# One core, a grouped-query decode step with a gated feed-forward branch: q turned on VectorE, whole-row products in the down and output projections, the first set reordered

## The chip, the cores and the metric

The kernel runs on one core of one Trainium2 chip. The metric is device time in microseconds (us) of one execution. The core has five engines with queues of their own: TensorE (PE in the profile, with its weight loads as PEld), VectorE (DVE), ScalarE (ACT), GpSimd (POOL) and SyncE (SP), which here issues every transfer. They meet only through semaphores.

## What is computed

One decode step for a batch of four, over 32 query heads in 8 groups and the last 4096 of 16384 cached positions, beside a gated feed-forward branch; a sigmoid mixes the two.

```python
g = sigmoid((x * gate_w).sum(-1, keepdims=True))            # x: 4 x 1 x 512
q = (x @ wq)                                                # 32 heads of 128
k, v = k_cache[:, :, Sk - W:, :], v_cache[:, :, Sk - W:, :] # W = 4096, 8 heads, each for 4 query heads
p = softmax(einsum("bhqd,bhkd->bhqk", q, k) * 128 ** -0.5)
a = einsum("bhqk,bhkd->bhqd", p, v).reshape(4, 1, 4096) @ wo
gate, up = x @ W_gate, x @ W_up                             # 512 x 1792
b = (gate * (gate > 0) * up) @ W_down                       # 1792 x 512
return g * a + (1 - g) * b
```

All inputs are bf16. K and V of the window are 67 MB of the 81 MB that are read.

## The kernel before

**Sets and slots.** The work is cut into eight sets, one batch row with four of the eight key heads each: 4 MB of K and 4 MB of V. SBUF has four slots of 4 MB. V always takes slot 3; wq, the K tiles, the gate and up weights, the down weights and wo take slots 0 to 2 in turn. `_dma_order` (L159) is the order on SyncE's queue: wq, x, gate_w, K0, K1, V0, and then K(s), V(s-1) pair by pair, the feed-forward weights around the last V, and wo in five pieces (`WO_PIECES`, L26, in units of half a row group of 256 columns). A load waits until its slot is free (`_slots`, L166): V(s) for the value product of set s-1, K for the scores of the K that lay there. Whatever stands behind a waiting issue waits too.

**The start.** Constants for masks and sums are made on POOL and TensorE (`CONST`). `XT` turns x on TensorE; `Z` is the product for the gate's sigmoid; `Q` is x @ wq in 32 products of four rows, four column groups side by side, into two banks. The rows of q must come to lie as block-diagonal weights `qblk`. Before, `EQ` (L554 on VectorE, L658 on ScalarE) copies each bank four times over, `QT` (L339) turns the result in 16 fp32 transposes on TensorE, and `EQT` (L564) puts it into place in 16 copies out of PSUM.

**A set.** VectorE transposes a quarter of K in 32x32 blocks (`EKT`, called KT in the order; 128x2048 as fp32 pairs); TensorE multiplies it with `qblk` (`SC`, eight products of 512 columns for a quarter); VectorE adds the mask, takes the maximum and writes the scores to SBUF (`ESC`, L584). After four quarters `MAX` and a small TensorE product (`SW`) give each row its maximum; ScalarE takes the exponential of all 2048 columns (`EXP`, L687); VectorE transposes the result (`EPT`, called PT, L599); TensorE forms the value product (`PV`, 32 products in two column groups); ScalarE copies it to `osb` (`NORM`, L672). VectorE's order is written out in `_order` (L148). TensorE's is a loop whose blocks are shared by all sets: scores of quarters 0 and 1, value product of the set before, scores of quarters 2 and 3, `SW`.

**The end.** `RS` sums the exponentials by row. `GU` multiplies x with the gate and up weights; RELU, `H` and `EHT` make the hidden activations and turn them. Then come the last value product, `FFN` (L408, down projection), `OQ` (L385, which folds the value products of all sets into the layout of the output projection by 16 products with 0/1 weights), `EOQ` (L608, scaling), and `WO` (L416). FFN and WO add into one PSUM bank: each row group of 512 output columns is two products of 256 columns, one in rows 0 to 3 and one in rows 64 to 67, in two column groups of the array. `FIN` copies both halves to SBUF and the result goes out.

The wait that orders the value tiles is this line of `_slots`:

```python
frees[n] = {"k": [("E", "SC", it[-1], 2)], "v": [("PV", it[-1])], "wq": [("Q", 1)], ...}[k]
```

Of the kernel before, what the change touches and what calls it, by code (L numbers as in the profile page):

```python
# [11 lines left out]
B = 4  # L12
# [12 lines left out]
OR = 128 // OUTT  # L25
WO_PIECES = ((0, 35), (35, 52), (52, 59), (59, 62), (62, 64))  # L26
# [78 lines left out]
def _alloc(nc, ctx):  # L105
# [13 lines left out]
    sb("osb", [128, NSET, 512], BF16)  # L119
    sb("oq", [128, 32, 4], BF16)  # L120
    sb("identb", [128, 128], BF16)
    sb("identf", [128, 128], FP32)
# [11 lines left out]
    sb("fold", [128, 4, 4, 64], BF16)  # L134
# [4 lines left out]
    sb("recip", [128, 4, 4], FP32)  # L139
# [8 lines left out]
def _order():  # L148
    o = [("CONST", k) for k in ("mask", "grp", "rfold")] + [("XT",), ("Z",), ("Q",), ("QT",), ("KT", 0, 0), ("KT", 0, 1), ("SC", 0, 0)]
    o += [("KT", 0, 2), ("SC", 0, 1), ("KT", 0, 3), ("SC", 0, 2), ("SC", 0, 3), ("SW", 0)]  # L150
    for s in range(1, NSET):
        o += [("KT", s, 0), ("KT", s, 1), ("PT", s - 1), ("SC", s, 0), ("KT", s, 2), ("SC", s, 1), ("KT", s, 3), ("PV", s - 1)]
# [35 lines left out]
def _program(nc, plan, R, aps):  # L188
# [3 lines left out]
    TR, SCB, ACC, OB = (0, 1), (2, 3), 5, 6  # L192
    slots, kt, sc, pe, pT, qblk = R["slots"], R["kt"], R["sc"], R["pe"], R["pT"], R["qblk"]
    xsb, xT, osb, oq = R["xsb"], R["xT"], R["osb"], R["oq"]
    identb, identf, ones = R["identb"], R["identf"], R["ones"]
# [17 lines left out]
    turns = [("CONST", k) for k in consts] + [("XT",)] + [("QT", n, x) for n in range(2) for x in range(2)]  # L213
    bank_of = {key: TR[i % 2] for i, key in enumerate(turns)}
    bank_of.update({("Q", 0): 2, ("Q", 1): 3, ("RS", 0): 0, ("RS", 1): 1, ("GU", 0): 2, ("GU", 1): 3, ("OQ",): 4})
# [4 lines left out]
    free = {("RS", 0): [("E", "SW", NSET - 1)], ("RS", 1): [], ("GU", 0): [("E", "SC", NSET - 1, 2)],  # L220
# [51 lines left out]
    def gpsimd(e):  # L272
# [12 lines left out]
        aff(identf[:, :], ones[:, :], [[-1, 128]], 0, eq, 0.0, ("IDF",))  # L285
# [11 lines left out]
        for g in range(8):  # L297
            v = R["fold"][:, g % 4, :, :]
            aff(v, v, [[1, 4], [-1, 64]], -64 * g, ne, 1.0, ("FOLD", g), mult=4)

    def tensor(t):
# [37 lines left out]
        def QT():  # L339
            for n in range(2):  # L340
                for x in range(2):
                    key = ("QT", n, x)
                    for y in range(4):
                        src = qd(n)[:, 512 * x + 128 * y:512 * x + 128 * y + 128]
                        tp(banks[tr(key)][:, 128 * y:128 * (y + 1)], src, identf[:, :], ev=key if y == 3 else None,
                           waits=tr_free(key) + [("QD", n), ("IDF",)])

# [19 lines left out]
        def RS(g):  # L367
            key = ("RS", g)
            mm(banks[tr(key)][:, 0:4], R["rfold"][:, :], rowsum[:, 4 * g:4 * g + 4], True, True, ev=key,
               waits=tr_free(key) + [("EXP", 4 * g + 3), ("E", "CONST", "rfold")])  # L370
# [14 lines left out]
        def OQ():  # L385
            key = ("OQ",)
            if plan.emit:
                E.take("nm", 1)
            for t in range(2):
                for cc in range(2):  # L390
                    for c in range(4):
                        x = 256 * t + 128 * cc + 32 * c
                        first, lastmm = (t, cc, c) == (0, 0, 0), (t, cc, c) == (1, 1, 3)
                        mm(banks[tr(key)][0:64, 0:256], R["fold"][:, 2 * cc + t, c, :], osb[:, :, x:x + 32], first, lastmm,
                           ev=key if lastmm else None, pos=(0, 0),
                           waits=tr_free(key) + [("FOLD", 7)] if first else ())

        def GU():
            for n, (W, key) in enumerate(((Wg, "WG"), (Wu, "WU"))):
# [8 lines left out]
        def FFN():  # L408
            for i in range(14):
                for j in range(OUTT):  # L410
                    x = 512 * i + OW * j
                    mm(banks[ACC][OR * j:OR * j + 4, 0:OW], R["hg"][:, i, :], Wd[:, x:x + OW], i == 0, False,
                       ev=("FFN",) if (i, j) == (13, OUTT - 1) else None, waits=[("E", "HT"), ("WD",), ("G",)],
                       pos=(0, OR * j))

        def WO(p):  # L416
            lo, hi = WO_PIECES[p]
            w = [("WO", p), ("E", "OQ")]
            for x in range(lo, hi):
                i, j = x // OUTT, x % OUTT  # L420
                mm(banks[ACC][OR * j:OR * j + 4, 0:OW], oq[:, i, :], Wo[:, OW * x:OW * x + OW], False, i == 31,
                   ev=("WOP", p) if x == hi - 1 else None, waits=w if x == lo else (), pos=(0, OR * j))

        fns = dict(CONST=CONST, XT=XT, Z=Z, Q=Q, QT=QT, SC=SC, PV=PV, SW=SW, RS=RS, OQ=OQ, WO=WO, GU=GU, FFN=FFN)
# [6 lines left out]
        def setup():  # L431
            run("CONST", "XT", "Z", "Q", "QT")
            E.wait([("E", "QT", n, 1) for n in range(2)] + [("E", "CONST", "grp")])

        if not plan.emit:
# [9 lines left out]
            run("FFN", "OQ", "WO")  # L445
# [38 lines left out]
        with block("mix"):  # L484
            run("FFN", "OQ")
            for p in range(len(WO_PIECES) - 1):
                WO(p)
            t.br("pe_tail")
# [6 lines left out]
    for it in order:  # L495
# [10 lines left out]
        elif k == "Q":  # L506
            dve += [("EQ", 0), ("G",)]
            act.append(("EQ", 1))
        elif k == "QT":
            dve += [("EQT", 0), ("EQT", 1)]  # L510
# [8 lines left out]
        elif k == "PT":  # L519
            dve.append(("EPT", it[1]))  # L520
        elif k == "RS":
            dve.append(("ERS", it[1]))
        elif k == "PV":
            act.append(("NORM", it[1]))
        elif k == "OQ":
            dve.append(("EOQ",))
    dve.append(("FIN",))
    act.append(("FIN",))

    def qd(n):  # L530
        return (pe, sc)[n][:, :].bitcast(FP32)

    def q_dst(n, u):
        return (pe, sc)[n][:, :].rearrange("p (x u w) -> p x u w", x=8, u=4)[:, :, u, :]

    def q_src(n):
        return banks[scb(("Q", n))].rearrange("p (x w) -> p x w", x=8)

    def vector(v):
# [14 lines left out]
        def EQ(n):  # L554
            key = ("Q", n)
            E.op(lambda: v.tensor_copy(q_dst(n, 0), q_src(n)), ev=("E",) + key, waits=[key])
            E.op(lambda: v.tensor_copy(q_dst(n, slice(1, 4)), bc(q_dst(n, slice(0, 1)), 2, 3)), ev=("QD", n),
                 waits=[("E",) + key])
# [5 lines left out]
        def EQT(n):  # L564
            U32 = mybir.dt.uint32
            keys = [("QT", n, x) for x in range(2)]
            assert [tr(k) for k in keys] == list(TR)
            src = R["psum"][:, 0:2, :].bitcast(U32).rearrange("p k (h g j b) -> p g b j (k h)", h=2, g=2, j=4)
            for q in range(4):
                r = slice(32 * q, 32 * q + 32)  # L570
                for g in range(2):
                    dst = qblk[r, 4 * n:4 * n + 4, g, 16 + 32 * q:32 + 32 * q, :].rearrange("p b c e -> p b (c e)")
                    dst = dst.bitcast(U32).rearrange("p b (j h) -> p b j h", j=4)
                    E.op(lambda dst=dst, r=r, g=g: v.tensor_scalar(dst, src[r, g, 0:B, :, :], 0, None, op0=ALU.bitwise_or),  # L574
                         ev=("E",) + keys[1] if (q, g) == (3, 1) else None, waits=keys + [("QZ",)])
            plan.ev[("E",) + keys[0]] = plan.ev[("E",) + keys[1]]

        def ESC(s, f):
            key = ("SC", s, f)
            w = [key]  # L580
            if f == 0:
                w += [("EXP", s - 1)] if s > 0 else [("QT", 1, 1)]
# [19 lines left out]
        def ERS(g):  # L602
            key = ("RS", g)
            E.op(lambda: v.reciprocal(recip[:, 2 * g, :], banks[tr(key)][:, 0:4]), ev=("E",) + key, waits=[key])
            E.op(lambda: v.tensor_tensor(recip[:, 2 * g + 1, :], recip[:, 2 * g, :], gg[:, 0, :], ALU.mult), ev=("RG", g),
                 waits=[("E",) + key, ("G",)])

        def EOQ():  # L608
            key = ("OQ",)
            for g in range(2):  # L610
# [4 lines left out]
                    bc(recip[0:64, 2 * g + 1, :].unsqueeze(2), 2, 32), ALU.mult), ev=("E",) + key if g else None,  # L615
                    waits=[key, ("RG", 1)])
# [16 lines left out]
        def FIN():  # L633
            E.op(lambda: v.tensor_copy(osum[:, OW:2 * OW], banks[ACC][OR:OR + 4, 0:OW]), ev=("OSUM", 1),  # L634
                 waits=[("WOP", len(WO_PIECES) - 1)])

        fns = dict(INIT=INIT, EKT=EKT, EXT=EXT, EQ=EQ, G=G, EQT=EQT, ESC=ESC, MAX=MAX, ESW=ESW, EPT=EPT, ERS=ERS, EOQ=EOQ, H=H,
# [15 lines left out]
    def scalar(a):  # L653
        E = _Eng(plan, a, "act")

        def EQ(n):
            key = ("Q", n)
            E.op(lambda: a.activation(q_dst(n, slice(0, 4)), bc(q_src(n).unsqueeze(2), 2, 4), ACTF.Copy), ev=("QD", n),  # L658
                 waits=[key])
            plan.ev[("E", "Q", n)] = plan.ev[("QD", n)]  # L660
# [10 lines left out]
        def NORM(s):  # L671
            E.op(lambda: a.activation(osb[:, s, :], ob, ACTF.Copy), ev=("NORM", s), ctr="nm",  # L672
# [54 lines left out]
```

## Time and profile before

| | before |
|---|---|
| median of three runs | 197.69 us (196.96 to 198.31) |
| profiled execution, its own time | 197.25 us |
| its span, first to last instruction | 196.0 us |
| mean granted TensorE clock | 0.852 |
| PE, PEld busy | 125.8, 56.4 us |
| DVE, ACT, POOL busy | 124.7, 27.5, 9.5 us |
| read from HBM | 81.01 MB, 413 GB/s over the span |

The page divides the span into 40 equal slices and gives for each the busy share of the engines, the granted clock, the share of the 16 DMA engines and the rate. A timeline row reads: start, length, engine, line, operation, output and input, shapes, count, and in brackets how long the engine was idle before it and what ended that. Rows of equal instructions are merged, so a length covers all of them. A row of windows gives, for a stretch, its length and each engine's busy time with its count (PE, PEld, DVE, ACT, POOL), then the granted clock, the DMA share and GB/s. Matmuls and transposes go through helpers, so all have line 305 or 309 and are told apart by their tiles.

### The profile page before, as it was taken

What the parts mean: (1) busy time and instruction counts of PE and PEld (TensorE: products, weight loads), DVE (VectorE), ACT (ScalarE), POOL (GpSimd) and SP (SyncE); (2) the same over time, 40 slices, a digit from 0 to 9 for tenths busy, and PEclk for the clock granted to TensorE, in tenths of its full rate; (3) what the DMA queues carried; (4) which work ended last, traced back from release to release, by engine and by line L of the source; (5) the groups of instructions that cost most, each with busy time, mean ns of one, the idle gap of its engine ahead of it and who ended that gap; (6) DMA issues with size and microseconds to landing.
All of it is one profiled execution on the core that took longest, in us unless ns stands there. A gap on an engine that the chain in (4) does not pass through costs nothing. (4 is left out here: it accounts for less than half of the span.)

```text
span 196.0 us, 2003 instructions
## 1 busy us (share of the span) xinstructions
PE 125.8 (64%) x723; PEld 56.4 (29%) x723; DVE 124.7 (64%) x153; ACT 27.5 (14%) x34; POOL 9.5 (5%) x25
## 2 busy tenths in 40 slices
PE   0209356649938963896389546954795589563976
PEld 0004212213413421252125212511251125221563
DVE  6103688699679949963995399539954994371010
ACT  2212100040140003011301120112012201220100
POOL 7830000000000000000000000000000000000000
PEclk9999859957996995799669978995899579965799
DMA  6999999999599999999999999999999999999994
GB/s 214 441 442 448 435 438 428 448 428 428 214 421 448 435 435 428 428 428 428 428 428 428 428 428 428 428 428 428 428 428 428 455 420 430 447 441 395 433 409 156
DMA packets 3619, 81.03 MB, mean 413 GB/s; under 512 B 409, under 2 KB 674, under 8 KB 802
## 3 DMA queue, kind: packets, MB, share of 16 engines
q1 hardware_dynamic: 3618, 81.01, 96.7%
q8 instruction: 1, 0.02, 0.0%
HBM read 81.01 MB, written 0.00 MB: 413 GB/s over the span
## 5 line engine op out<-in xcount | busy, mean ns | idle before, releaser
L305 PE MATMUL bank<-kt,qblk 128*128 128x512 bf16 x256 | 75.0, 455 | 30.6 <-PEq L82 30.6
L548 DVE STREAM_TRANSPOSE kt<-slots 128x2048 f32<-128x2048 f32 x32 | 72.9, 2297 | 4.2 <-DMA slots<-in_A_k_cache_dram 4.1
L305 PEld LDWEIGHTS bank<-kt,qblk 128*128 x256 | 27.8, 111 | 74.2 <-issue 57.3
L584 DVE CUSTOM_DVE_ANT_0 sc<-bank,maskf 128x512 bf16<-128x512 f32 x32 | 21.5, 671 | 28.2 <-PE bank L305 28.2
L305 PE MATMUL bank<-slots,pT 128*64 128x512 bf16 x256 | 31.0, 397 | 10.9 <-PEq L82 10.9
L305 PEld LDWEIGHTS bank<-slots,pT 128*64 128x64 bf16 x256 | 16.8, 114 | 25.4 <-issue 16.8
L687 ACT ACTIVATE pe<-sc,negmax 128x2048 bf16<-128x2048 bf16 x8 | 16.0, 2002 | 50.7 <-DVE negmax L594 50.7
L599 DVE STREAM_TRANSPOSE pT<-pe 128x2048 bf16<-128x2048 bf16 x8 | 18.2, 2274 | 2.2 <-ACT pe L687 2.2
L672 ACT ACTIVATE osb<-bank 128x512 bf16<-128x512 f32 x8 | 4.8, 597 | 91.2 <-PE bank L305 91.2
L612 DVE TENSOR_TENSOR oq<-bank,recip 64x128 bf16<-64x128 f32 x2 | 0.9, 432 | 11.4 <-PE bank L305 11.4
L305 PE MATMUL bank<-rd,grpb 128*128 128x32 bf16 x8 | 1.4, 176 | 8.9 <-PEq L82 8.9
L305 PE MATMUL bank<-slots,xT 128*4 128x512 bf16 (+1 forms) x64 | 6.3, 564 | 0.0
L552 DVE COPY xT<-bank 128x20 bf16<-128x20 bf16 x1 | 0.2, 171 | 8.0 <-PE bank L309 8.0
L305 PE MATMUL bank<-slots,oq 128*4 128x256 bf16 x64 | 4.4, 272 | 1.1 <-DVE oq L612 1.1
L574 DVE TENSOR_SCALAR qblk<-bank 32x64 uint32<-32x64 uint32 x16 | 2.9, 215 | 3.0 <-PE bank L309 2.9
L305 PE MATMUL bank<-maskr,maskl 128*128 128x512 bf16 x1 | 0.6, 607 | 5.9 <-POOL maskr L281 5.9
L305 PEld LDWEIGHTS bank<-rd,grpb 128*128 128x128 bf16 x8 | 0.8, 96 | 12.6 <-issue 12.6
L309 PE MATMUL bank<-identb,xsb 5*128 5x5 bf16 x4 | 0.3, 168 | 5.9 <-DMA xsb<-in_gate_w_dram 5.9
L305 PEld LDWEIGHTS bank<-slots,oq 128*4 128x4 bf16 x64 | 2.7, 84 | 2.9 <-DMA slots<-in_A_wo_dram 2.4
L281 POOL TENSOR_SCALAR_AFFINE_SELECT fold<-fold 128x256 bf16<-128x256 bf16 x8 | 3.3, 417 | 1.1
L594 DVE TENSOR_REDUCE negmax<-bank 128x1 f32<-128x32 f32 x8 | 1.5, 191 | 2.9 <-PE bank L305 2.9
L634 DVE CAST xsb<-bank 4x256 bf16<-4x256 f32 x1 | 0.4, 419 | 4.6 <-PE bank L305 4.6
(59 smaller groups left out, 42.2 us busy)
## 6 DMA issues: line engine op xcount, KB each, us to landing
slots<-in_A_k_cache_dram SPq DMA_DIRECT2D x8, 4096.0 KB, 24.8
slots<-in_A_v_cache_dram SPq DMA_DIRECT2D x8, 4096.0 KB, 15.6
slots<-in_A_wq_dram SPq DMA_DIRECT2D x1, 4096.0 KB, 12.3
slots<-in_A_wo_dram SPq DMA_DIRECT2D x1, 2240.0 KB, 21.6
slots<-in_B_W_gate_dram SPq DMA_DIRECT2D x1, 1792.0 KB, 19.3
slots<-in_B_W_up_dram SPq DMA_DIRECT2D x1, 1792.0 KB, 23.0
slots<-in_B_W_down_dram SPq DMA_DIRECT2D x1, 1792.0 KB, 18.2
slots<-in_A_wo_dram SPq DMA_DIRECT2D x1, 1088.0 KB, 23.8
```

Of the source, the lines that this page charges most:

```text
L281: op(lambda: e.affine_select(dst, src, pattern, cmp, fill, base=base, channel_multiplier=mult), ev)
L305: E.op(lambda: t.matmul(out_, lhsT, rhs, start=start, stop=stop, tile_position=pos, skip_group_check=True), ev=ev, waits=waits)
L309: E.op(lambda: t.transpose(out_, in_, idn), ev=ev, waits=waits)
L548: E.op(lambda: v.transpose(kt[:, f % 2, :].bitcast(FP32), slot("k", s)[:, 4096 * f:4096 * f + 4096].bitcast(FP32)), ev=("E", "KT", s, f), ...
L574: E.op(lambda dst=dst, r=r, g=g: v.tensor_scalar(dst, src[r, g, 0:B, :, :], 0, None, op0=ALU.bitwise_or), ev=("E",) + keys[1] if (q, g) == ...
L584: E.op(lambda: v.tensor_tensor_reduce(sc[:, 512 * f:512 * f + 512], banks[scb(key)], R["maskf"][:, :], 1.0, -3.0e38, ALU.add, ALU.max, mx4 ...
L594: E.op(lambda: v.tensor_reduce(negmax[:, s % 2:s % 2 + 1], banks[tr(key)][:, 0:32], AXIS.X, ALU.min), ev=("E",) + key, waits=[key])
L599: E.op(lambda: v.transpose(pT[:, :], pe[:, :]), ev=("E", "PT", s), ctr="pt", waits=[("EXP", s)] + ([("PV", s - 1)] if s else []))
L612: E.op(lambda g=g, r=r: v.tensor_tensor(oq[r, :, :].rearrange("p i b -> p b i"), banks[tr(key)][0:64, 128 * g:128 * g + 128].rearrange("p ...
L634: E.op(lambda: v.tensor_copy(osum[:, OW:2 * OW], banks[ACC][OR:OR + 4, 0:OW]), ev=("OSUM", 1), waits=[("WOP", len(WO_PIECES) - 1)])
L672: E.op(lambda: a.activation(osb[:, s, :], ob, ACTF.Copy), ev=("NORM", s), ctr="nm", waits=[("PV", s)])
L687: E.op(lambda: a.activation(pe[:, :], sc[:, :], ACTF.Exp, bias=negmax[:, s % 2:s % 2 + 1], scale=SCALE, accum_out=rowsum[:, s:s + 1]), ev= ...
```

## The change

**q on VectorE.** Each bank of Q is copied once to bf16 (ScalarE one, VectorE one), transposed in 32x32 blocks as fp32 pairs (`TQ`), and put into `qblk` by 32 copies of 32x32 elements (`QB`). The 16 TensorE transposes, the fourfold copies and the fp32 identity are gone. `Q` goes ahead of `Z`, and `G` (the sigmoid's reciprocal) moves behind the first `EPT`.

**The first set.** The next set's first K transpose is put ahead of the first set's last score block, its maximum and `SW`.

**The fold.** `NORM` now packs the two halves of a set that matter into `osb` of half the width, in four copies of 32 rows; for the last set ScalarE does two and VectorE two. `OQ` needs 8 products instead of 16. `RS` is one product instead of two.

**Whole rows.** `FFN` forms 14 products of 512 columns in rows 0 to 3 of a bank of its own instead of 28 halves, and the first 12 of 32 row groups of wo (`WX`) likewise. The other 20 stay in halves: the left ones are added to the same rows 0 to 3, the right ones go to rows 64 to 67 of the old bank. So the right half of FFN and WX is copied aside (`XS`) before the left halves start, and added in `FIN`. In the first piece of wo all right halves go ahead of the left ones. `OQ` stands ahead of `FFN`. `GU` waits for the last `EPT`.

TensorE's program has 449 instructions in place of 551, weight loads and products counted apart.

```diff
-    o = [...] + [("XT",), ("Z",), ("Q",), ("QT",), ("KT", 0, 0), ("KT", 0, 1), ("SC", 0, 0)]
-    o += [("KT", 0, 2), ("SC", 0, 1), ("KT", 0, 3), ("SC", 0, 2), ("SC", 0, 3), ("SW", 0)]
+    o = [...] + [("XT",), ("Q",), ("Z",), ("KT", 0, 0), ("KT", 0, 1), ("SC", 0, 0)]
+    o += [("KT", 0, 2), ("SC", 0, 1), ("KT", 0, 3), ("SC", 0, 2)]
     for s in range(1, NSET):
-        o += [("KT", s, 0), ("KT", s, 1), ("PT", s - 1), ("SC", s, 0), ...]
+        o += [("KT", s, 0)] + [("SC", 0, 3), ("SW", 0)] * (s == 1) + [("KT", s, 1), ("PT", s - 1), ("SC", s, 0), ...]
...
-    o += [("PT", s), ("RS", 0), ("RS", 1), ("GU",), ("PV", s), ("FFN",), ("OQ",)]
+    o += [("PT", s), ("RS",), ("GU",), ("PV", s), ("OQ",), ("FFN",), ("WX",)]
...
         def GU():
+            if plan.emit:
+                E.take("pt", 1)
...
         def FFN():
             for i in range(14):
-                for j in range(OUTT):
-                    x = 512 * i + OW * j
-                    mm(banks[ACC][OR * j:OR * j + 4, 0:OW], R["hg"][:, i, :], Wd[:, x:x + OW], i == 0, False, ...)
+                mm(banks[ACX][0:4, :], R["hg"][:, i, :], Wd[:, 512 * i:512 * i + 512], i == 0, False, ...)
+
+        def WX():
+            for i in range(WHOLE):
+                mm(banks[ACX][0:4, :], oq[:, i, :], Wo[:, 512 * i:512 * i + 512], False, i == WHOLE - 1, ...)
 
         def WO(p):
             lo, hi = WO_PIECES[p]
-            for x in range(lo, hi):
+            xs = list(range(max(lo, OUTT * WHOLE), hi))
+            if p == 0:
+                xs.sort(key=lambda x: -(x % OUTT))
+            for n, x in enumerate(xs):
                 i, j = x // OUTT, x % OUTT
-                mm(banks[ACC][OR * j:OR * j + 4, 0:OW], oq[:, i, :], Wo[:, OW * x:OW * x + OW], False, i == 31, ...)
+                w = [("WO", p), ("E", "OQ")] if n == 0 else [("XS",)] if p == 0 and j == 0 else []
+                mm(banks[(ACX, ACC)[j]][OR * j:OR * j + 4, 0:OW], oq[:, i, :], Wo[:, OW * x:OW * x + OW], (i, j) == (WHOLE, 1), i == 31, ...)
...
+        def TQ(n):
+            E.op(lambda: v.transpose(qcol(n).bitcast(FP32), qrow(n).bitcast(FP32)), ev=("TQ", n), waits=[("QR", n)])
+
+        def QB():
+            src = sc[:, 0:1024].bitcast(U32).rearrange("p (n g h w) -> p n w h g", n=2, g=4, h=2)
+            for u in range(4):
+                r = slice(32 * u, 32 * u + 32)
+                for j in range(4):
+                    dst = qblk[r, :, :, 16 + 32 * u + 4 * j:20 + 32 * u + 4 * j, :].rearrange("p s h c e -> p s h (c e)").bitcast(U32)
+                    for n in range(2):
+                        E.op(lambda: v.tensor_scalar(dst[:, 4 * n:4 * n + 4, :, :], src[32 * j:32 * j + 32, n, 0:B, :, :], 0, None, op0=ALU.bitwise_or), ...)
...
         def FIN():
-            E.op(lambda: v.tensor_copy(osum[:, OW:2 * OW], banks[ACC][OR:OR + 4, 0:OW]), ...)
+            E.op(lambda: v.tensor_tensor(osum[:, OW:2 * OW], banks[ACC][OR:OR + 4, 0:OW], R["xs"][OR:OR + 4, :], ALU.add), ...)
...
+        def XS():
+            E.op(lambda: a.activation(R["xs"][OR:OR + 4, :], banks[ACX][0:4, OW:2 * OW], ACTF.Copy), ev=("XS",), waits=[("WX",)])
```

More of the change, by code (lines that the diff above doesn't have):

```diff
@@ L138, in _alloc @@
     sb("rowsum", [128, NSET], FP32)
-    sb("recip", [128, 4, 4], FP32)
+    sb("recip", [128, 2, 8], FP32)
     sb("ge", [128, 2, 4], FP32)
@@ L387, in OQ @@
             if plan.emit:
-                E.take("nm", 1)
+                E.take("nm", 2)
             for t in range(2):
[L390 to L396, printed above, removed]
+                for c in range(4):
+                    x = 128 * t + 32 * c
+                    mm(banks[tr(key)][0:64, 0:256], R["fold"][:, t, c, :], osb[:, :, x:x + 32], (t, c) == (0, 0), (t, c) == (1, 3),
+                       ev=key if (t, c) == (1, 3) else None, pos=(0, 0), waits=[("FOLD", 7)] if (t, c) == (0, 0) else ())
         def GU():
+            if plan.emit:
+                E.take("pt", 1)
             for n, (W, key) in enumerate(((Wg, "WG"), (Wu, "WU"))):
@@ L431, in setup @@
         def setup():
-            run("CONST", "XT", "Z", "Q", "QT")
-            E.wait([("E", "QT", n, 1) for n in range(2)] + [("E", "CONST", "grp")])
+            run("CONST", "XT", "Q", "Z")
+            E.wait([("QB",), ("E", "CONST", "grp")])
         if not plan.emit:
@@ L444, in tensor @@
             PV(NSET - 1)
-            run("FFN", "OQ", "WO")
+            run("OQ", "FFN", "WX", "WO")
             return
@@ L656, in EQ @@
         def EQ(n):
[L657 to L660, printed above, removed]
+            E.op(lambda: a.activation(qrow(n), banks[scb(("Q", n))], ACTF.Copy), ev=("QR", n), waits=[("Q", n)])
         def ECONST(k):
@@ L671, in NORM @@
         def NORM(s):
-            E.op(lambda: a.activation(osb[:, s, :], ob, ACTF.Copy), ev=("NORM", s), ctr="nm",
-                 waits=[("PV", s)])
+            parts = ((0, 0), (1, 0), (0, 1), (1, 1))
+            norm(E, lambda d, p: a.activation(d, p, ACTF.Copy), s, parts[0:2 if s == NSET - 1 else 4], "NORM")
         def GE():
```

132 lines of the change are left out of this document (59 added, 73 removed).

## The prediction

> **What bounds the kernel now.** I read the page's picture of the span first, then the chain that ended last.
>
> ```profile
> GB/s 214 441 442 448 435 438 428 448 428 428 214 421 448 435 435 428 428 428 428 428 428 428 428 428 428 428 428 428 428 428 428 455 420 430 447 441 395 433 409 156
> q1 hardware_dynamic: 3618, 81.01, 96.7%
> DMA slots<-in_A_wo_dram 12%; PE bank L305 4%; DVE sc L584 0%; DVE xsb L634 0%; SPq L242 0%; DVE mx L584 0%
> ```
>
> 81 MB come in at a flat 428 to 448 GB/s with one hole, slice 11 of 40. No engine is near that load; only the hole, the first transfer and what follows the last can move the end. The issues on SyncE's queue in order of time:
>
> ```profile
> 0.80 0.39 SPq L242 DMA_DIRECT2D slots<-in_A_wq_dram  x1
> ...
> 1.93 1.25 SPq L242 DMA_DIRECT2D slots<-in_A_k_cache_dram  x2
> 3.22 0.61 SPq L242 DMA_DIRECT2D slots<-in_A_v_cache_dram  x1
> ...
> 51.74 0.54 SPq L242 DMA_DIRECT2D slots<-in_A_v_cache_dram  x1
> ...
> 87.46 0.54 SPq L242 DMA_DIRECT2D slots<-in_A_v_cache_dram  x1
> ...
> 106.89 0.53 SPq L242 DMA_DIRECT2D slots<-in_A_v_cache_dram  x1
> ```
>
> From 87.46 to 106.89 one K and one V (4096 KB each) take 19.43 us, so 9.71 us per load. The second V waits for its only slot until 51.74, the end of the first set's value product. Windows of 1 us around it (last two columns: DMA share, GB/s):
>
> ```profile
> 50.00:51.00 1.00, 1.00 (x12) 0.56 (x10) 1.00 (x1) 0.00 (x0) 0.00 (x0) 1.00 0.46 197
> 51.00:52.00 1.00, 1.00 (x10) 0.33 (x6) 0.82 (x1) 0.26 (x1) 0.00 (x0) 1.00 0.08 33
> 52.00:53.00 1.00, 1.00 (x7) 0.43 (x5) 0.00 (x0) 0.34 (x1) 0.00 (x0) 1.00 0.00 0
> 53.00:54.00 1.00, 1.00 (x6) 0.43 (x5) 0.42 (x1) 0.00 (x0) 0.00 (x0) 1.00 1.20 426
> ```
>
> The queue runs dry near 51.0; the load issued at 51.74 brings data from about 53.1, 1.4 us after its issue. To leave no hole, the issue must come by 51.0 - 1.4 = 49.6. The hole's worth comes from the landings (K tiles, then V tiles, then one DMA window from 28 to 32 us):
>
> ```profile
> DMA to landing us min/median/max: 20.9/24.8/34.5
> DMA to landing us min/median/max: 12.5/15.6/40.1
> q8 instruction: 1, 0.02, 1.6%
> ```
>
> The first K lands at 1.93 + 20.9 = 22.8, the first V (the 40.1) at 3.22 + 40.1 = 43.3, the second V (the 12.5) at 51.74 + 12.5 = 64.2. At 9.71 per load the first V was due at 22.8 + 19.4 = 42.2: 1.1 late. One packet of code, 0.02 MB, lies in that stretch; 1.6% of 16 engines over 4 us is 1.0 us of one engine, and each load needs all sixteen. The second V was due at 43.3 + 19.4 = 62.7: 1.5 late, the hole. Together **2.6 us** that data could come earlier. At the other end:
>
> ```profile
> 172.38 2.31 DVE L599 STREAM_TRANSPOSE pT<-pe 128x2048 bf16<-128x2048 bf16 x1 [2.16 <-ACT pe L687]
> 172.72 2.67 PE L305 MATMUL bank<-slots,xT 128*4 128x448 bf16 x32
> 179.79 5.46 PE L305 MATMUL bank<-slots,pT 128*64 128x512 bf16 x32 [4.40 <-PEq L82]
> 185.18 1.69 PE L305 MATMUL bank<-slots,gwB 128*4 128x256 bf16 x28
> 186.80 1.93 PE L305 MATMUL bank<-osb,fold 128*64 128x256 bf16 x16
> 188.77 0.88 DVE L612 TENSOR_TENSOR oq<-bank,recip 64x128 bf16<-64x128 f32 x2 [11.39 <-PE bank L305]
> 189.80 4.42 PE L305 MATMUL bank<-slots,oq 128*4 128x256 bf16 x64 [1.06 <-DVE oq L612]
> 191.97 0.85 PEld L305 LDWEIGHTS bank<-slots,oq 128*4 128x4 bf16 x17 [0.34 <-DMA slots<-in_A_wo_dram]
> 193.94 0.08 PEld L305 LDWEIGHTS bank<-slots,oq 128*4 128x4 bf16 x2 [0.21 <-DMA slots<-in_A_wo_dram]
> 194.26 0.37 ACT L691 ACTIVATE xsb<-bank 4x256 bf16<-4x256 f32 x1 [8.37 <-PE bank L305]
> 194.26 0.42 DVE L634 CAST xsb<-bank 4x256 bf16<-4x256 f32 x1 [4.60 <-PE bank L305]
> ```
>
> The last value product starts as its V lands, at 179.8; from its end at 185.2 TensorE hardly stops, and pieces two to five of wo find it waiting a few tenths each. The tail is 194.26 - 185.18 = 9.1 us, balanced between landings and TensorE, so work added there shows at once.
>
> **The change part by part: the start.** Rows of the first set:
>
> ```profile
> 13.73 0.17 DVE L552 COPY xT<-bank 128x20 bf16<-128x20 bf16 x1 [8.04 <-PE bank L309]
> 14.88 3.58 PE L305 MATMUL bank<-slots,xT 128*4 128x512 bf16 x32
> 22.78 1.47 DVE L574 TENSOR_SCALAR qblk<-bank 32x64 uint32<-32x64 uint32 x8 [1.19 <-PE bank L309]
> 24.28 4.50 DVE L548 STREAM_TRANSPOSE kt<-slots 128x2048 f32<-128x2048 f32 x2
> 35.96 0.65 DVE L584 CUSTOM_DVE_ANT_0 sc<-bank,maskf 128x512 bf16<-128x512 f32 x1
> 38.12 0.69 DVE L584 CUSTOM_DVE_ANT_0 sc<-bank,maskf 128x512 bf16<-128x512 f32 x1 [1.49 <-PE bank L305]
> 39.19 0.18 PE L305 MATMUL bank<-rd,grpb 128*128 128x32 bf16 x1 [1.11 <-PEq L82]
> 42.12 6.01 PE L305 MATMUL bank<-kt,qblk 128*128 128x512 bf16 x16 [2.75 <-PEq L82]
> 48.06 3.64 PE L305 MATMUL bank<-slots,pT 128*64 128x512 bf16 x32
> 51.74 0.60 ACT L672 ACTIVATE osb<-bank 128x512 bf16<-128x512 f32 x1 [10.02 <-PE bank L305]
> ```
>
> Q now precedes Z: it starts when xT is there and wq has landed, at 13.95 instead of 14.88, and ends near 17.5. Then one 128x512 copy on ScalarE (0.60 by the 51.74 row), one transpose of an eighth of the 4.50/2 = 2.25 us one (0.3), so 18.5. The 32 small copies have no row: 32x32 elements out of SBUF. The nearest copies twice the elements out of PSUM in 1.47/8 = 0.18; half of it, 0.09, is my lower end, 0.22 (0.18 without overlap) the upper. I take 0.14, as overhead doesn't halve: 32 x 0.14 = 4.5, qblk ready at 23.0. The first K is there at 22.8, so its transposes start near 23.1: **1.2 earlier** (1.4 at the low end, bound by the landing; 1.3 later at the high end, 18.5 + 7.0 = 25.5).
>
> The reorder puts the next K's first transpose (2.25) where VectorE stood for 1.49. The fourth score block, the maximum and its TensorE step come 0.8 later, but that step (39.19, now 40.0) is followed at once by the next set's scores, which before began at 42.12: 2.1 earlier. They need the second transpose, which now stands behind the maximum at 40.3 and ends near 42.6; at the old 5.9 us they end near 46.0, 2.0 earlier. The transposed weights, 2.3 behind 42.6 at 44.9, and the V at 42.2 are there. The K that the moved transpose waits for landed at 22.8 + 9.7 + 1.1 = 33.6, before 36.6, so nothing queued behind it on VectorE waits. The value product ends at 51.7 - 1.2 - 2.0 = **48.5**, 1.1 inside 49.6. The hole closes; late next is the queue itself, which then holds the following K. The high end gives 51.0 and a hole of 1.4.
>
> The code packet goes if TensorE's program called for it, which shrinks from 551 instructions to 449, counting weight load and product apart; all other programs are under 200. No row names whose code it is. Between gone (1.1) and kept (0) I take gone, as one packet in a whole span fits the one long program. Then no engine of the sixteen lags. Start: **-2.6**, with -1.2 as the end if the copies are slow.
>
> At no price: the split NORM, four quarter copies near 0.4 (the rows at 194.26) instead of one of 0.60, on a ScalarE that stood idle 10.02 before it; one row-sum product instead of two; the moved G; fewer constants on POOL. GU now waits for the last transposed weights, 172.38 + 2.31 = 174.7 instead of 172.7; behind it on TensorE stands only the value product, which waits for V until 179.8, 2.4 after GU's new end. RELU, H and the h transpose follow 2 us later, and FFN needs them only in the tail.
>
> **The tail**, from the end of the last value product. A 512-column product at full clock: the row at 48.06 has 32, two column groups side by side, in 3.64; less 0.07, by which FFN's row overlaps the next one's start, that is 3.57/16 = 0.223 for 512 columns. A pair of 256-column halves takes 2 x 1.62/28 = 0.116. FFN of 14 whole products therefore loses its pairing: 14 x 0.223 = 3.1 against 1.6.
>
> - NORM in two halves on two engines, now awaited: two of about 0.4 each (rows at 194.26) and the wake-up, 0.95; before, FFN covered it.
> - fold, 8 instead of 16: 0.97. Its evacuation, before 1.06 of waiting, now lies beside FFN.
> - FFN 3.1; WX 12 x 0.223 = 2.7; the other 11 of piece one, unpaired, 1.2, and 0.15 of waiting for XS (0.37, beside 5 products).
> - the last 29 halves, landed by then, 29 x 0.058 = 1.7.
>
> Sum 9.8 + 1.0 = 10.8 against 9.1: **+1.7**, bounds +0.8 (NORM, XS and gaps at half) and +2.3 (the final add 0.2 dearer than its cast, 0.4 more gaps).
>
> Clock: the value product took 5.46 where 3.64 is full speed. Windows, the column before the last two being the granted clock:
>
> ```profile
> 175.00:180.00 5.00, 0.60 (x8) 0.21 (x4) 2.03 (x5) 0.00 (x0) 0.00 (x0) 0.50 1.02 438
> 180.00:185.00 5.00, 5.00 (x32) 2.44 (x28) 0.00 (x0) 0.00 (x0) 0.00 (x0) 0.65 0.98 416
> ```
>
> Half clock, until well inside the product. All at half clock would be 2 x 3.57 = 7.1, all at full 3.6: -1.8 to +1.7 on a tail that no longer hides it. I take no change. [...]
>
> Sum: -2.6 + 1.7 = -0.9. Against the profiled execution's own 197.25 (span 196.0 and 1.25 around it) 196.4; against the median, 197.69, which is 0.44 above, 196.8. I say **196.6**.
>
> **Rivals.**
>
> *The tail hides its work* (chance 0.15): the value product runs at full clock, since GU ends 2.4 instead of 4.4 us before it, and landings set the end again. For it: the shorter idle. Against: GU's 2.7 us are themselves at half clock. All of 2.6 stays: 195.1.
>
> *The code packet stays or comes elsewhere* (0.15): only the 1.5 of the hole are won, against 1.7: +0.2, 197.5 to 197.9. For it: only one packet shows, not what calls for it. [...]
>
> *Slower: the copies eat the lead* (0.12). If each of the 32 costs over (24.2 - 18.5)/32 = 0.18, the hole starts to reopen; from (24.28 + 2.0 - 18.5)/32 = 0.24 it is as before, the lag hides in it again, and the tail's 1.7 is left: 199.0 on the profile, 199.4 on the median, over 199.7 with a colder value product. For it: they have no row. Against: 0.18 is the price of twice the elements.
>
> **How the numbers follow.** Forecast 0.55, rivals 0.15, 0.15, 0.12, others 0.03. The forecast's own range is 0.9 below (tail at its lower bound) and 1.4 above (the slow copies' hole): 195.7 to 198.0. The first rival widens it to 195.2 below; above, the second lies inside and the third is left out: 195.2 to 198.2. About 1%, 2 us, is what a measurement can tell from no change. Faster by it, under 195.7: the first rival and a little of the forecast, 0.22. Slower, over 199.7: 0.09. Within: 0.69.
>
> **What would show it.** No hole near slice 11; V loads still 19.4 apart but the second issued before 49.6; no q8 packet; first K transpose near 23; the copies near 0.14; FFN about 3.1 us for 14; no wait on wo in the last 29 products. It is wrong if the second V is issued after 50, if a code packet shows, or if the last products wait for wo.

## The result, and the profile after

The changed kernel takes 198.40 us (median of 20 runs, 197.38 to 199.14); the kernel before, run beside it, 197.04 us (20 runs, 195.9 to 199.8). The ratio is 1.0068, with a 95% interval of 1.0046 to 1.0091: slower by 0.7%, where 196.6 was forecast, 0.6% under the 197.69 of the three runs that the prediction had.

Yet the profiled execution's span is shorter, 195.4 us against 196.0. Its time is 197.93: 2.5 us lie outside the span, where before it was 1.25. The gain in the span is only that over one of the longer executions before: over all runs its median is 195.45 for the changed kernel, and 195.0 to 195.4 for the kernel before in the groups of runs below. By medians the span has not become shorter, and the loss lies outside it: 2.78 us against 1.25. The page of the changed kernel, its span in 40 slices, the queues, and the chain that ended last:

```profile
span 195.4 us, 1939 instructions
...
GB/s 215 429 430 449 436 429 443 456 431 429 396 429 436 436 436 429 429 443 436 429 443 429 429 429 429 429 429 436 429 429 429 429 402 428 457 429 409 428 387 28
...
q8 instruction: 1, 0.02, 0.0%
q14 instruction: 1, 0.01, 0.0%
...
PE bank L305 7%; DVE osb L606 0%; DVE xsb L634 0%; ACT xs L688 0%
```

The hole in slice 11 is all but gone (396 instead of 214, with 429 on both sides). No transfer is left in the chain: from the last value product on it is TensorE's work. And two packets of code lie in the span instead of one. The start of the changed kernel in order of time (the second V and the third K on SyncE's queue are the last two rows):

```profile
18.33 4.67 DVE L572 TENSOR_SCALAR qblk<-sc 32x32 uint32<-32x32 uint32 x32
23.04 4.50 DVE L548 STREAM_TRANSPOSE kt<-slots 128x2048 f32<-128x2048 f32 x2
...
38.80 0.18 PE L305 MATMUL bank<-rd,grpb 128*128 128x32 bf16 x1 [1.74 <-PEq L83]
...
39.58 3.89 PE L305 MATMUL bank<-kt,qblk 128*128 128x512 bf16 x16 [0.60 <-PEq L83]
...
43.98 3.64 PE L305 MATMUL bank<-slots,pT 128*64 128x512 bf16 x32 [0.51 <-PEq L83]
...
47.65 0.54 SPq L243 DMA_DIRECT2D slots<-in_A_v_cache_dram  x1
...
48.23 0.60 SPq L243 DMA_DIRECT2D slots<-in_A_k_cache_dram  x1
```

The second V is issued 4.1 us earlier than before. Where the code packets ran, by windows of the transfers (40 to 44 us, then 192 us to the end of the span):

```profile
q14 instruction: 1, 0.01, 0.5%
```

```profile
q8 instruction: 1, 0.02, 1.9%
```

The first is new, 0.3 us of one DMA engine (0.5% of 16 engines over 4 us). The second is the 16 KB packet: it was in the window from 28 to 32 before and now runs when the last products are done; it is through half a microsecond before the last instruction ends. The record reaches past the span, and there, in a window from 196 to 200 us, lies one packet more:

```profile
q14 instruction: 1, 0.01, 0.7%
```

Narrow windows put its start between 197.7 and 197.8, 2.3 us behind the last instruction. The kernel before has no packet there.

The landings of V after their issues (the largest is the first V), and then, in a window from 45 to 60 us, the second V alone:

```profile
DMA to landing us min/median/max: 14.5/15.6/39.7
```

```profile
slots<-in_A_v_cache_dram SPq DMA_DIRECT2D x1, 4096.0 KB, 14.7
```

The first V lands at 3.22 + 39.7 = 42.9, 0.7 late instead of 1.1; the second at 47.65 + 14.7 = 62.3 instead of 64.2. So 1.9 us were won by then in this execution, not 2.6. The tail:

```profile
177.91 5.17 PE L305 MATMUL bank<-slots,pT 128*64 128x512 bf16 x32 [1.88 <-PEq L83]
...
183.12 0.76 ACT L670 ACTIVATE osb<-bank 32x256 bf16<-32x256 f32 x2 [7.99 <-PE bank L305]
183.12 0.86 DVE L606 CAST osb<-bank 32x256 bf16<-32x256 f32 x2 [5.09 <-PE bank L305]
...
184.04 1.06 PE L305 MATMUL bank<-osb,fold 128*64 128x256 bf16 x8 [0.95 <-DVE osb L606]
...
185.03 3.18 PE L305 MATMUL bank<-slots,gwB 128*4 128x512 bf16 x14
...
188.05 2.75 PE L305 MATMUL bank<-slots,oq 128*4 128x512 bf16 x17
190.84 0.37 ACT L688 ACTIVATE xs<-bank 4x256 f32<-4x256 f32 x1 [6.96 <-PE bank L305]
...
191.26 2.35 PE L305 MATMUL bank<-slots,oq 128*4 128x256 bf16 x35 [0.46 <-ACT xs L688]
...
193.65 0.42 DVE L634 TENSOR_TENSOR xsb<-bank,xs 4x256 bf16<-4x256 f32 x1 [7.63 <-PE bank L305]
```

From the end of the value product (183.1) to the final add it is 10.5 us, against 9.1 before. The last products no longer wait for wo: the row at 191.26 names `XS`.

### The profile page after: what moved, and what is told of

Read it like the earlier page. It is cut to its first block, busy times and chain, and to the rows that moved or that the text cites. A ratio compares the mean times of both kernels' runs of the same rounds, so it can differ in the third digit from the quotient of the medians.

```text
span 195.4 us, 1939 instructions
## 1 busy us (share of the span) xinstructions
PE 123.3 (63%) x671; PEld 53.3 (27%) x671; DVE 127.1 (65%) x170; ACT 33.0 (17%) x57; POOL 8.8 (4%) x24
## 5 line engine op out<-in xcount | busy, mean ns | idle before, releaser
L305 PE MATMUL bank<-kt,qblk 128*128 128x512 bf16 x256 | 73.9, 448 | 32.0 <-PEq L83 31.9
L670 ACT ACTIVATE osb<-bank 32x256 bf16<-32x256 f32 x30 | 11.2, 374 | 86.7 <-PE bank L305 86.4
L305 PEld LDWEIGHTS bank<-slots,pT 128*64 128x64 bf16 x256 | 17.5, 114 | 24.5 <-issue 16.4
L305 PE MATMUL bank<-slots,oq 128*4 128x256 bf16 (+1 forms) x52 | 5.1, 297 | 0.5 <-ACT xs L688 0.5
L572 DVE TENSOR_SCALAR qblk<-sc 32x32 uint32<-32x32 uint32 x32 | 4.5, 177 | 0.2
L606 DVE CAST osb<-bank 32x256 bf16<-32x256 f32 x2 | 0.8, 424 | 5.1 <-PE bank L305 5.1
```

The costliest lines, as they stand in the source:

```text
L305: E.op(lambda: t.matmul(out_, lhsT, rhs, start=start, stop=stop, tile_position=pos, skip_group_check=True), ev=ev, waits=waits)
L572: E.op(lambda: v.tensor_scalar(dst[:, 4 * n:4 * n + 4, :, :], src[32 * j:32 * j + 32, n, 0:B, :, :], 0, None, op0=ALU.bitwise_or), ev=("QB ...
L606: norm(E, lambda d, p: v.tensor_copy(d, p), s, ((0, 1), (1, 1)), "NORMV")
L670: norm(E, lambda d, p: a.activation(d, p, ACTF.Copy), s, parts[0:2 if s == NSET - 1 else 4], "NORM")
```

## The experiments

The theory after the result: part of TensorE's code is now fetched at the very end instead of in mid-kernel (the 16 KB packet starts at 193.9 us, before at 29.2), and the execution can't end before it; the rest is the longer tail, paid for by the closed hole. Rivals: VectorE's and ScalarE's longer programs, or the new end itself. For each kernel below, "over the span" is a run's time less its own span, the median over its runs. The kernels ran in three groups, each on a chip of its own with the kernel before beside it: the first four below (before: 196.69 us), the next four (196.55) and the last three (196.54).

**The code made long again, executed** (all else as changed):

```diff
-            run("CONST", "XT", "Q", "Z")
+            run("CONST")
+            if plan.emit:
+                for _ in range(102):
+                    t.reg_alu(half, half, 2, op=ALU.bitwise_xor)
+            run("XT", "Q", "Z")
```

> The changed kernel with 102 register instructions that do nothing put into TensorE's program between the constants and the turn of x, where TensorE waits about 6 us for a transfer anyway: 551 instructions again, all else as changed. Theory (code at the end): in the profile of the changed kernel the 16 KB code packet of queue q8 runs at 193.9 us, when the last products are done, instead of 29.2, and the time lies 2.5 us over the span instead of 1.25. With the long program the packet is back near 29, the time lies about 1.3 us over the span, and the kernel takes about 197.0, near the kernel before. Rival (the longer programs of VectorE and ScalarE, or the new end itself, cost it): still 2.5 us over the span, 198.4.

Measured: 199.08 us, ratio to the kernel before 1.0119 (1.0064 to 1.0174); 1.50 over the span (6 runs). The extra microseconds over the span went, as the theory said, but the time did not follow: the register instructions held up the turn of x, which began at 16.74 instead of 13.06, the second V was issued at 51.95, and the hole was back. A 16 KB packet ran at 31.7 and another at 196.7, past the span's end at 197.3, which the theory had not foreseen. A spoiled test of the time, kept for its packets.

**VectorE's and ScalarE's programs made as long as in the changed kernel** (the kernel before):

```diff
             v.reg_mov(left, 0)
+            for _ in range(20):
+                v.reg_alu(left, left, 2, op=ALU.bitwise_xor)
...
+        for n in range(22):
+            E.op(lambda: a.activation(R["spare"][:, n:n + 1], R["ones"][:, 0:1], ACTF.Copy), waits=[("ONES",)])
```

> The kernel before with 20 idle register instructions more for VectorE and 22 tiny copies more for ScalarE, ahead of their work, so that both programs are as long as in the changed kernel; TensorE's stays at 551. Theory (TensorE's code at the end): time and span as before, 197.0 and some 1.2 us over the span. Rival (VectorE's or ScalarE's length): about 2.5 us over the span, 198.3.

Measured: 197.55 us, ratio 1.0054 (1.0018 to 1.0089), 1.42 over the span. So these programs do not make the 2.8. But the 8 KB packet near 41 us appears in this kernel, and so does one 1.2 us behind the last instruction; the kernel before has neither. The kernels of this document that have the late one are those with some 56 operations on ScalarE, 1.42 us or more over the span; those with 34 have none, 1.25 to 1.30. The runs of this kernel scatter from 196.2 to 198.9, and the 0.5% can't be given to one cause.

**The start alone** (the kernel before with the new `Q`, `TQ`, `QB` and the new order; its hunks stand in the diff above).

> The kernel before with only the start of the change: q turned on VectorE, Q ahead of Z, the first set reordered, G moved. The tail is the old one; TensorE's program has 520 instructions. Theory: the hole near 51 us closes, the second V is issued near 47.7, a code packet still runs in mid-kernel and keeps one of the sixteen DMA engines about 1 us late, so 1.5 us of the 2.6 are won, and the time lies about 1.2 us over the span: about 195.5. Rival (start worth nothing, or the time over the span grows with VectorE's longer program): 196.8 or more.

Measured: 195.94 us (12 runs, 195.68 to 196.29) against 196.69 (29 runs, 195.68 to 198.62 but for one of 232.6): ratio 0.9952 (0.9924 to 0.998). The issue of the second V, at 47.90, and the code packet in mid-kernel are as the theory said; of the time only half was won, 0.75 us of the expected 1.5. The baseline shows why 1.5 was too much to expect of the median: **the kernel before is that fast in its best runs.** Its times spread over 2.9 us, those of this kernel over 0.6. That the hole is smaller in its shorter runs is likely, but not shown, as only one of its executions was profiled. The nearest is the kernel with the lengthened programs, whose first set is the same: in an execution of 196.17 us its second V was issued at 50.52, and slice 11 held 276 GB/s.

**Halves again** (the changed kernel):

```diff
-                mm(banks[ACX][0:4, :], R["hg"][:, i, :], Wd[:, 512 * i:512 * i + 512], i == 0, False, ...)
+                for j in range(OUTT):
+                    x = 512 * i + OW * j
+                    mm(banks[ACC][OR * j:OR * j + 4, 0:OW], R["hg"][:, i, :], Wd[:, x:x + OW], i == 0, False, ...)
...
-    o += [("PT", s), ("RS",), ("GU",), ("PV", s), ("OQ",), ("FFN",), ("WX",)]
+    o += [("PT", s), ("RS",), ("GU",), ("PV", s), ("OQ",), ("FFN",)]
```

> The changed kernel with the down projection and all of wo in halves of 256 columns as before (28 and 64 products), one bank, no copy aside; shorter fold, the order fold before down projection and the split copy stay. TensorE's program has 501 instructions. Theory: the tail from the end of the last value product is about 9.1 to 9.3 us instead of 10.5, but the code still comes at the end, 2.5 us over the span: span near 194.1, time near 197.0. Rival (the whole-row products cost nothing, the awaited copy does): tail 10.3 or more, time 198.2.

Measured: 196.07 us, ratio 0.9956 (0.9924 to 0.9988); span 194.6, over the span 1.45. The expectation was wrong twice: with 501 instructions the code packet was back in mid-kernel (30.6), and the tail is not 9.1 to 9.3 us but 10.8, as long as the rival said, at a time that the rival excluded. The tail, by the timeline of this kernel:

```profile
178.47 3.64 PE L305 MATMUL bank<-slots,pT 128*64 128x512 bf16 x32 [1.90 <-PEq L83]
...
183.06 1.06 PE L305 MATMUL bank<-osb,fold 128*64 128x256 bf16 x8 [0.95 <-DVE osb L599]
...
184.05 1.69 PE L305 MATMUL bank<-slots,gwB 128*4 128x256 bf16 x28
...
188.00 2.13 PE L305 MATMUL bank<-slots,oq 128*4 128x256 bf16 x35 [2.25 <-DMA slots<-in_A_wo_dram]
...
190.69 2.15 PE L305 MATMUL bank<-slots,oq 128*4 128x256 bf16 x29 [0.56 <-DMA slots<-in_A_wo_dram]
...
192.88 0.42 DVE L627 CAST xsb<-bank 4x256 bf16<-4x256 f32 x1 [7.83 <-PE bank L305]
```

Of the 10.8 us TensorE waits 2.25 and 0.56 for wo, so the short fold, the awaited copy and the new order hide: the span is 194.6 as in the start alone (194.7). It is the whole rows that pushed TensorE past the transfers.

**Dead code** (the changed kernel; the block is never entered):

```diff
-            t.br("pe_tail")
+            t.br_lt(at, 0, on_true="pe_pad", on_false="pe_tail")
+        with block("pad"):
+            for _ in range(50):
+                t.reg_alu(half, half, 2, op=ALU.bitwise_xor)
+            t.br("pe_tail")
```

> The changed kernel with 50 instructions between the fourth and the last piece of wo that a branch always skips: TensorE's program is 500 long again, its last block lies as far back as in the run with the halves, and nothing more is executed. Theory (where the program ends decides when the code behind it is fetched): the 16 KB packet runs near 30 us, not at the end, the time lies 1.4 us over the span instead of 2.8, and as the tail of whole rows stays 1.3 us longer than that of the halves (196.07), 197.3. Rival (what is executed at the end costs it, not the program's length): 2.8 us over the span, 198.4.

Measured: 196.98 us (12 runs, 196.69 to 197.53), ratio 1.0001 (0.9973 to 1.0029). The span is that of the changed kernel (median 195.55 against 195.45); over the span it is 1.43 instead of 2.78. Its window from 28 to 32 us:

```profile
q8 instruction: 1, 0.02, 1.6%
```

Fifty instructions that nobody executes make the kernel 1.4 us faster, all of it after the span. The 12 runs lie between 1.27 and 1.55 over the span, the 20 of the changed kernel between 2.34 and 3.60. That settles the place and the size of the larger part: it hangs on the length of TensorE's program, or on where its last block then lies, and not on what it computes. The edit also puts a conditional branch in place of a plain one; the kernels with 389 instructions (below) and 501 (above) have the plain branch and 1.44 and 1.45, so it isn't that.

**The kernel before without the branch hint**:

```diff
-        here = t.mark_branch_hint_location()
-            t.br_lt(at, 0, on_true="pe_tail", on_false="pe_end").branch_hint(here)
+            t.br_lt(at, 0, on_true="pe_tail", on_false="pe_end")
```

> The kernel before without the one branch hint in TensorE's program (the hint names the never-taken branch at the end of the program); 550 instructions. Theory (the hint fetches the end of the program early, since the end lies in a block of code of its own): no packet of queue q8 near 29 us, one near the end instead, the time about 2.5 us over the span, no late DMA engine after 29 us: about 198. Rival (code is fetched in order whatever the hint says): packet near 29 us and 196.7 as before.

Measured: 196.35 us, ratio 0.9983 (0.9946 to 1.002), 1.29 over the span. Both are wrong in part: the packet near 28 us is still there, so the hint does not bring it, and a second one runs at 193.2, which costs nothing that shows. So a packet at the end does not by itself lengthen the time; the kernels with the long time outside the span are those whose only 16 KB packet runs at the end.

**The two halves of the start**, each alone on the kernel before: the order alone, and the turn of q alone.

> The kernel before with the first set reordered and nothing else: q still turned on TensorE. By the prediction's terms the second V is issued 2.0 us earlier, near 49.7, just when the queue runs dry: the hole is nearly closed, the late DMA engine decides, 195.9 to 196.4, and the times scatter less than the kernel before's (195.7 to 198.6). Rival (the turn of q is what closes the hole): still a hole of about 1 us, 196.7 with the old scatter.

> The kernel before with q turned on VectorE, Q ahead of Z and G moved, but the first set in its old order. By the prediction's terms the second V is issued 1.2 us earlier, near 50.5: some 0.9 us too late, so part of the hole is left, about 196.3, scattering. Rival (q alone closes it): 195.9 and no scatter.

Measured: the order alone 196.10 us, ratio 0.9973 (0.9937 to 1.0008); q alone 197.59 us, ratio 1.0048 (1.001 to 1.0086). The first scores of the second set and the issue of the second V, order alone and then q alone:

```profile
40.88 5.32 PE L305 MATMUL bank<-kt,qblk 128*128 128x512 bf16 x16 [0.60 <-PEq L82]
...
49.81 0.54 SPq L242 DMA_DIRECT2D slots<-in_A_v_cache_dram  x1
```

```profile
41.36 6.40 PE L303 MATMUL bank<-kt,qblk 128*128 128x512 bf16 x16 [2.75 <-PEq L82]
...
51.37 0.54 SPq L241 DMA_DIRECT2D slots<-in_A_v_cache_dram  x1
```

The order alone brings the issue to 49.8 (49.7 by the prediction's terms). q alone was to bring 50.5 and brings 51.4 in its profile: the scores began 0.8 earlier and took 6.40 instead of 6.01, and much of the lead was gone; with both edits the same 16 products took 3.89. The granted clock (the third figure from the end) tells the two cases apart, by windows of the kernel before, of q alone and of the changed kernel:

```profile
40.00:45.00 5.00, 2.88 (x7) 1.08 (x8) 5.00 (x3) 1.72 (x2) 0.00 (x0) 0.51 1.05 452
```

```profile
40.00:45.00 5.00, 3.64 (x9) 1.37 (x10) 5.00 (x3) 0.96 (x2) 0.00 (x0) 0.52 1.00 428
```

```profile
41.00:45.00 4.00, 3.41 (x21) 1.44 (x20) 3.96 (x7) 0.33 (x2) 0.00 (x0) 1.00 1.00 428
```

So the terms of the start do not add up one by one: which of TensorE's products run at half clock (0.51 and 0.52 here, against 1.00) shifts. It isn't the edits alone that decide it: with the same start these 16 products took 5.32 in the halves and 5.22 with the dead code. And why the median of q alone is 0.5% above that of the kernel before stays open. The kernel with the lengthened programs is slower by as much, and has the 8 KB packet near 41 and a hole as well. Two of twelve runs of the order alone still took 197.8 and 198.2.

**Shorter code still, and a length in between** (the changed kernel): 2 of GU's 32 products, most gate and up rows left out; and the dead block with 24 instructions instead of 50.

```diff
-                for q in range(4):
-                    for j in range(4):
-                        mm(banks[scb(fill)][32 * j:32 * j + 4, 0:448], xT[:, 5 * q:5 * q + 4], W[:, x:x + 448], ...)
+                mm(banks[scb(fill)][0:4, 0:448], xT[:, 0:4], W[:, 0:448], True, True, ...)
```

> The changed kernel with 2 of GU's 32 products (the gate and up rows are mostly left out; they run beside waiting, so the tail keeps its length): TensorE's program has 389 instructions. Theory (the code behind the program, too, must fit with it in what is loaded at the start): at 389 no 16 KB packet runs at all, the time lies 1.3 us over the span, about 196.9. Rival (every program that gets by without the packet near 30 us pays it at the end): packet near 193, 2.8 us over the span, 198.4.

> The changed kernel with 24 instructions that a branch always skips, 474 in all: between 449 (packet at the end, 198.4) and 500 (packet near 30 us, 197.0). It must fall to one of the two, and nothing else may differ: either packet near 30 us and 197.0, or at the end and 198.4. [...]

Measured: 389 instructions give 197.31 us (ratio 1.0029, 1.0 to 1.0057), no 16 KB packet at all, 1.44 over the span: the theory's outcome, not the rival's. That the code has to fit in what is loaded at the start was the author's guess, and no run shows it. 474 give 197.43 us (1.0046, 1.0008 to 1.0084), one packet at 31.7 and one at 195.2, 1.45 over the span. By its time this kernel lies between the two expected values, nearer 197.0, and both intervals overlap that of the changed kernel; it is outside the span that these two stand with the long programs. All lengths side by side, each on the changed kernel but for the last row; the last column is where a packet of 8 KB starts behind the last instruction:

| TensorE's instructions | 16 KB packets at | median us | over the span | 8 KB packet behind the end |
|---|---|---|---|---|
| 389 (most of GU left out) | none | 197.31 | 1.44 | 1.5 |
| 449 (as changed) | 193.9 | 198.40 | 2.78 | 2.3 |
| 474 (24 dead) | 31.7, 195.2 | 197.43 | 1.45 | 1.3 |
| 500 (50 dead) | 30.4 | 196.98 | 1.43 | 1.3 |
| 551 (102 executed) | 31.7, 196.7 | 199.08 | 1.50 | 1.3 |
| 551 (the kernel before) | 29.2 | 196.69 | 1.25 | none |

Only the length of the change as drawn pays at the end. The added microsecond lies between the last instruction and the 8 KB packet, and no record tells what fills it. The transfer of the 16 KB packet does not: it is through at 194.9, before the last instruction, while those at 195.2 (474) and 196.7 (551) run past the span's end and cost nothing that shows. Nor is such an execution unknown elsewhere: 7 of the 87 runs of the kernel before, and single runs of five other kernels, lie over 2 us outside the span too. In the changed kernel, with and without GU's wait (next), every run does.

**GU without its wait** (the changed kernel):

```diff
-            if plan.emit:
-                E.take("pt", 1)
```

> The changed kernel without GU's wait for the last transposed weights, so that GU runs 2 us earlier. The prediction put the wait at nothing: then 198.4, as the changed kernel. Rival (the wait keeps TensorE's clock up for the last value product): that product takes longer, up to 5.9 us instead of 5.2, and the time is 198.8 or more.

Measured: 198.93 us (6 runs), ratio 1.0107 (1.0066 to 1.0148), 2.67 over the span, beside 1.44 and 1.45 on the same chip; so the long time outside the span is not one chip's. Its last value product took 5.71:

```profile
171.00 2.18 PE L305 MATMUL bank<-slots,xT 128*4 128x448 bf16 x32
...
178.07 5.71 PE L305 MATMUL bank<-slots,pT 128*64 128x512 bf16 x32 [4.89 <-PEq L83]
```

The product and the time lie where the rival put them, but the interval overlaps that of the changed kernel (1.0046 to 1.0091) and the product's length is one execution's. The wait may be worth some tenths; it is not shown.

## Why the prediction was wrong

**The start, right in its mechanism.** Q begins at 13.6 (13.95 was said), the 32 copies cost 4.67/32 = 0.146 each (0.14), the first K transpose starts at 23.04 (23.1), the small product comes at 38.8 and the next scores 0.8 behind it, the second V is issued at 47.65 (48.5, and 49.6 as the limit). The last is earlier than said because the 16 products took 3.89 and not the old 5.9; where they took 5.2 to 5.3, with the dead code and in the halves, it came at 48.3. The hole is closed. The rival of the slow copies is out.

**What the start is worth: the first step that failed, and the largest.** The sum took -2.6 for it, 1.5 for the hole and 1.1 for the code packet. The 1.5 were read from one execution, and that one belongs to the slower half of the kernel before. Run beside it, the start alone wins 0.75 us of the median (196.69 to 195.94) and keeps a code packet near 30. The prediction carried a loss of the profiled execution to the median unchanged.

**The time outside the span and the code packet: the second step that failed.** The sum took the 1.25 us outside the span as fixed, and nothing stood against the shorter program. The dead-code run shows that term at 198.40 - 196.98 = 1.4 us (2.78 against 1.43 outside the span), with the sign of a loss. "Between gone (1.1) and kept (0) I take gone" had a third case: the packet moved to the end, one of the prediction's own signs of being wrong. The rival "the code packet stays or comes elsewhere" named the event but gave it the price of a late DMA engine, and that the packet makes the 1.4 is not shown either (see the table). Nor was the 1.1 won. Without a 16 KB packet ahead of it the first V landed at 42.7 to 43.1 (three kernels), with one at 43.2 to 43.6 (ten), against the 42.2 that the prediction called due: about 0.4 of the 1.1 goes with that packet, and the rest was there without it. An 8 KB packet at 41 us, 0.3 us long, came in its place; that it holds V up is not shown. Four kernels with the longer VectorE program (the lengthened one, the start alone, q alone, halves again) have that packet; the kernel before and the order alone have none.

Of what a code packet costs the runs show this: one in mid-kernel goes with 0.4 us of a late V, and three kernels with a 16 KB packet at the end lie 1.29 to 1.50 us over the span. That 449 instructions cost 1.4 us at the end is shown; what is waited for there stays open. The theory that code behind the program has to be fetched before the engines can finish was only argued.

**The tail, about right in one execution.** Predicted 10.8 us from the end of the value product, found 10.5; whole FFN 3.18 (3.1); the awaited copy, 183.12 to 184.04, 0.92 (0.95). Against halves, with the 16 KB packet in the same place in both (30.4 and 30.6), the whole rows cost 196.98 - 196.07 = 0.9 us of the median; the prediction's +1.7 was against a tail that ran 9.1, and in the halves with the new start 2.8 us of waiting for wo take its place. The rival that the tail hides its work is out: no wait for wo is left in the chain. The clock, taken as unchanged, nearly was: 5.17 us for the last value product at a granted clock of 0.70, after 5.46 at 0.66. That it would be so was the author's estimate, and no run shows it to hold: in the profiles of the other kernels the product took from 3.64 us (halves) to 5.71 (GU without its wait).

**The sum as it came out,** by medians: start -0.75, fold and order +0.13 (195.94 to 196.07), whole rows +0.9, time outside the span +1.4, together +1.7 on 196.69: 198.4. The sum closes by construction, since each term is the step from one median to the next, over different chips; side by side the loss was 1.36. Against the prediction's own terms the start is short by 1.85, the tail 0.7 cheaper, and the 1.4 stood nowhere. The start and the whole rows almost cancel, and what shows is the time outside the span.

The start alone beats both kernels, by 0.5% beside the kernel before and by 1.2% against the changed kernel's median. Its runs lie within 0.6 us, those of the changed kernel within 1.8.

## What to carry to other kernels

When a change alters the length of a program, look at the code packets in the trace and at the time outside the span, not at the span alone: an edit that shortens the code can lengthen what lies behind the last instruction, as here from 1.43 (500 instructions) to 2.78 (449). Before a hole in a transfer is priced from one profile, run the kernel often enough to see how far its times spread and where the profiled one lies among them. And work added behind the last transfers is free only up to the wait that stands there: here halves left 2.25 us of it in one profile and whole rows none.

## What the runs showed that was not expected

Fifty instructions that are never executed made a kernel 1.4 us faster (198.40 to 196.98). The program of 449 instructions takes 2.78 us outside the span, and those of 389 and 474 take 1.44 and 1.45. And the start alone took more scatter out of the times than length: the kernel before ran from 195.68 to 198.62 on one chip (but for one run of 232.6), the start alone from 195.68 to 196.29. A closed hole is not enough for that, though: with 24 dead instructions the second V was issued at 47.89, and the runs still spread from 196.66 to 199.28 on another chip.
